# Linear attention and a rational feed-forward layer: the reciprocal in PSUM, ScalarE ahead of VectorE, low parts on GpSimd

## The chip, the cores and the metric

The kernel runs on one NeuronCore of a Trainium2 chip. A core has a matrix engine (TensorE, PE in the profile; PEld is its weight load), three elementwise engines (VectorE or DVE, ScalarE or ACT, GpSimd or POOL), and SyncE (SP), which here only issues transfers. SBUF is the working memory, PSUM the memory that TensorE writes to, in eight banks of 128 x 512 float32. Each engine runs its own instructions in order and waits for others on semaphores. The metric is the device time of one execution in microseconds (us); lower is better.

## The reference

Linear attention over 8 batches of 576 tokens and 8 heads of 64, RMS-normed, then a feed-forward layer whose activation is a rational function. `P / Q` is taken for each of 4608 x 2048 values of h.

```python
kv = np.einsum('bhsd,bhse->bhde', k, v)
out = np.einsum('bhsd,bhde->bhse', q, kv)
rms = np.sqrt(np.mean(out * out, axis=-1, keepdims=True) + 1e-06)
x = (out / rms * g_norm)            # then (B*S, H*D) = (4608, 512)
...
h = x @ w_in                        # 512 -> 2048
h2 = h * h
h3 = h2 * h
P = a[0] + a[1] * h + a[2] * h2 + a[3] * h3
Q = 1.0 + np.abs(b[0]) * np.abs(h) + np.abs(b[1]) * h2
g = P / (Q + 1e-06)
return g @ w_out                    # 2048 -> 512
```

## The kernel before

**Tiles and chunks.** The 4608 tokens are nine tiles of 512 (`t`), the 2048 columns of h are sixteen chunks of 128 (`c`). One chunk is: `gemm1` (h = w_in chunk times x, 128 x 512 in a PSUM bank of the pool `h`, two banks), the elementwise part `ew_a` to `ew_d`, and `gemm2` (g times the chunk of w_out, added into four banks `acc`). The main loop walks over all 144 chunks; chunk i issues `gemm2` of chunk i - 2 (`LAG`) and `gemm1` of chunk i + 1, so TensorE is one chunk ahead of the elementwise engines and takes their results two chunks later. `finish` does the last chunk in two halves and stores the last tile.

**Plain and split.** In tile 0 (and, for w_out, in chunks 12 to 15 of tile 1: `unsplit`, `LATE`) matmuls run on plain float32. Elsewhere every operand is split into a high part, cast to fp32r by ScalarE, and a low part, the difference, which VectorE computes; three fp32r matmuls (high x low, low x high, high x high) take the place of one plain one. So g has `gh`, `gl` (L461, L462), x has `xh`, `xl` (L268, L272), q has `qh`, `ql` (L307, L316), and the weights have `wh`, `wl` (L224, L231).

**Weights.** They come as float64 words. VectorE and ScalarE convert them in units of two chunks (`conv_a`, `conv_b1`, `conv_b2`) during tile 0, and `split_w` splits them from chunk 14 of tile 0 on. The table `schedule` says in which chunk, counted through from 0, each unit is fetched, converted and split (its four numbers); 33 and 35 are chunks 1 and 3 of tile 2.

**The elementwise part.** ScalarE takes Square of h, |b0 h| and the inner polynomial's first step from PSUM; VectorE makes Q - 1 (`q`, L429), then u (L431, L437); ScalarE makes an estimate d of the reciprocal as exp(-ln Q) (L438, L439); VectorE does a Newton step with it (L443, L445, L451), which gives g. The scale and shift constants are [128, 1] columns.

**The order.** It is the order in which the code is written, per engine (`manual_schedule`). `ew_b` and `ew_c` have places (`fill`, -1 to 2) where VectorE takes up other work: conversions and splits of weights, x's low parts, and the steps of the next tile's attention, which run one per chunk (`attention`: `att_kv`, `att_o`, then `att_ms`, `att_rstd`, `att_rd`, `att_rb`, `att_norm`). In chunk 14 of each tile x of the next tile is split. All fetches and nearly all stores are issued by SyncE. The eight PSUM banks are four `acc`, two `h`, one `at` and one `ms`.

Of the kernel before, what the change touches and what calls it, by code (L numbers as in the profile page):

```python
# [23 lines left out]
def linear_attention_then_rational_ffn(  # L24
# [189 lines left out]
    def split_w(u):  # L214
        kind, c = u
        i = units.index(u)
        w = ups.pop(u)
# [6 lines left out]
        ACT.copy(wh, w)  # L224

        def rest():
            wl = gpart(0, 0) if i == 0 else fpart(i if i == NU - 1 else i - 1, "l")
            for j in range(2):
# [2 lines left out]
            DVE.tensor_tensor(wl, w, f32(wh), ALU.subtract)  # L231
        return rest
# [189 lines left out]
    def ew_a(t, c, ph, w=TW):  # L422
        nm = f"{t}_{c}"
        d = work.tile([P, w], F32, tag="d", name=f"d_{nm}")
# [2 lines left out]
        ACT.activation(d, ph, AF.Square)  # L427
        ACT.activation(q, ph, AF.Abs, scale=b0)  # L428
        DVE.scalar_tensor_tensor(q, d, b1abs, q, ALU.mult, ALU.add)  # L429
        ACT.activation(u, ph, AF.Identity, bias=na[:, 2:3], scale=na[:, 3:4])  # L430
# [1 line left out]
        pend[t, c] = (d, q, u)

    def ew_b(t, c, ph, fill=lambda k: None):
        d, q, u = pend[t, c]
# [2 lines left out]
        ACT.activation(d, q, AF.Ln, bias=bias[:, 2:3], scale=QSC)  # L438
        ACT.activation(d, d, AF.Exp, bias=bias[:, 3:4], scale=-1.0)  # L439

    def ew_c(t, c, fill=lambda k: None):
        d, q, u = pend[t, c]
        DVE.scalar_tensor_tensor(q, q, QEPS, d, ALU.add, ALU.mult)  # L443
# [1 line left out]
        DVE.scalar_tensor_tensor(u, u, na[:, 0:1], d, ALU.add, ALU.mult)  # L445
# [5 lines left out]
        DVE.scalar_tensor_tensor(g, q, 2.0, u, ALU.subtract, ALU.mult)  # L451
        fill(2)

    def ew_d(t, c, w=TW):
        u = pend.pop((t, c))[2]
# [6 lines left out]
        DVE.tensor_tensor(gl, u, f32(gh), ALU.subtract)  # L462
# [211 lines left out]
```

## Time and profile before

| | us |
|---|---|
| median of 3 runs (lowest, highest) | 917.36 (917.17, 919.2) |
| span of the profiled execution, first to last instruction | 915.9 |
| busy: PE, DVE, ACT, POOL | 899.0, 800.2, 685.3, 4.6 |
| mean granted TensorE clock | 0.994 |

The page lists no time of the profiled execution other than its span; the three timed runs lie 1.3 to 3.3 us above it. A row of the timeline has the start, the length, the engine, the line, the operation and out<-in by the program's names; in brackets the idle time of the engine before it and what ended it. A row of the waits has who waited, for whom, and the total, the number and the longest. A group's row has the count, the busy time, the mean in ns, and the idle time before.

### The profile page before, as it was taken

What the parts mean: (1) busy time and instruction counts of PE and PEld (TensorE: products, weight loads), DVE (VectorE), ACT (ScalarE), POOL (GpSimd) and SP (SyncE); (2) the same over time, 40 slices, a digit from 0 to 9 for tenths busy, and PEclk for the clock granted to TensorE, in tenths of its full rate; (3) what the DMA queues carried; (4) which work ended last, traced back from release to release, by engine and by line L of the source; (5) the groups of instructions that cost most, each with busy time, mean ns of one, the idle gap of its engine ahead of it and who ended that gap; (6) DMA issues with size and microseconds to landing.
All of it is one profiled execution on the core that took longest, in us unless ns stands there. A gap on an engine that the chain in (4) does not pass through costs nothing.

```text
span 915.9 us, 11648 instructions
## 1 busy us (share of the span) xinstructions
PE 899.0 (98%) x4292; PEld 679.7 (74%) x4292; DVE 800.2 (87%) x1251; ACT 685.3 (75%) x1163; POOL 4.6 (1%) x32
## 2 busy tenths in 40 slices
PE   7999999999999999999999999999999999999998
PEld 5444445777678788878887888788887888788886
DVE  3799999999988899889987997889878988898887
ACT  2687866988687778777877787678867787777665
POOL 2000000000000000000000000000000000000000
PEclk7999999999999999999999999999999999999999
DMA  8946101221032013211221113120212020101001
GB/s 314 373 172 226 34 25 41 92 76 48 1 127 70 18 42 103 65 41 47 87 81 41 48 41 126 42 48 29 98 52 48 0 69 13 48 1 46 1 1 46
DMA packets 24992, 65.89 MB, mean 72 GB/s; under 512 B 2856, under 2 KB 3880, under 8 KB 24936
## 3 DMA queue, kind: packets, MB, share of 16 engines
q1 hardware_dynamic: 23328, 63.58, 21.5%
q10 hardware_dynamic: 1608, 1.58, 0.5%
q8 instruction: 33, 0.54, 0.3%
q14 instruction: 23, 0.19, 0.1%
HBM read 55.58 MB, written 9.57 MB: 71 GB/s over the span
## 4 chain that ended last, share of the span: by engine, by line
PE 83%; DVE 11%; ACT 3%; issue 2%; DMA 1%; ACTq 0%; DVEq 0%
PE h L417 13%; PE h L419 12%; PE h L418 12%; PE acc L478 11%; PE acc L479 11%; PE acc L480 11%; PE acc L474 3%; PE h L413 2%; PE kvp L301 2%; DVE q L429 1%; DVE u L445 1%; DVE q L443 1%; PE idle L533 1%; DVE u L437 1%; PE ms L345 1%
## 5 line engine op out<-in xcount | busy, mean ns | idle before, releaser
L427 ACT ACTIVATE d<-h 128x512 f32<-128x512 f32 x143 | 85.7, 599 | 160.6 <-PE h L419 146.9
L417 PE MATMUL h<-x,parts 128*128 128x512 f32 (+1 forms) x516 | 205.8, 399 | 0.0
L419 PE MATMUL h<-x,parts 128*128 128x512 f32 (+1 forms) x516 | 200.5, 389 | 0.0
L479 PE MATMUL acc<-wol,gh 128*128 128x512 f32 x492 | 191.6, 389 | 0.7 <-DVE wol L231 0.7
L429 DVE SCALAR_TENSOR_TENSOR q<-d,b1abs,q 128x512 f32<-128x512 f32 x143 | 107.1, 749 | 81.5 <-ACT q L428 81.2
L418 PE MATMUL h<-x,wil 128*128 128x512 f32 (+1 forms) x452 | 175.5, 388 | 0.0
L478 PE MATMUL acc<-parts,gl 128*128 128x512 f32 x440 | 171.6, 390 | 0.2 <-DVE gl L462 0.2
L480 PE MATMUL acc<-parts,gh 128*128 128x512 f32 x440 | 171.2, 389 | 0.0
L438 ACT ACTIVATE d<-q,bias 128x512 f32<-128x512 f32 x143 | 105.4, 737 | 29.9 <-DVE q L429 28.8
L417 PEld LDWEIGHTS h<-x,parts 128*128 128x128 f32 x516 | 96.9, 188 | 26.4 <-DVE gl L462 5.0
L419 PEld LDWEIGHTS h<-x,parts 128*128 128x128 f32 x516 | 96.9, 188 | 20.6
L430 ACT ACTIVATE u<-h,na 128x512 f32<-128x512 f32 x143 | 112.0, 783 | 0.0
L479 PEld LDWEIGHTS acc<-wol,gh 128*128 128x128 f32 x492 | 92.4, 188 | 20.0 <-DVE wol L231 1.0
L439 ACT ACTIVATE d<-d,bias 128x512 f32<-128x512 f32 x143 | 103.5, 724 | 4.6
L445 DVE SCALAR_TENSOR_TENSOR u<-u,na,d 128x512 f32<-128x512 f32 x143 | 106.5, 745 | 0.0
L437 DVE SCALAR_TENSOR_TENSOR u<-u,na,h 128x512 f32<-128x512 f32 x143 | 106.0, 741 | 0.3
L443 DVE SCALAR_TENSOR_TENSOR q<-q,d 128x512 f32<-128x512 f32 x143 | 98.4, 688 | 1.3 <-ACT d L439 1.3
L431 DVE TENSOR_TENSOR u<-u,h 128x512 f32<-128x512 f32 x143 | 97.8, 684 | 0.9
L428 ACT ACTIVATE q<-h,ab 128x512 f32<-128x512 f32 x143 | 98.1, 686 | 0.0
L418 PEld LDWEIGHTS h<-x,wil 128*128 128x128 f32 x452 | 85.0, 188 | 16.2 <-issue 0.2
L478 PEld LDWEIGHTS acc<-parts,gl 128*128 128x128 f32 x440 | 82.6, 188 | 18.5 <-DVE gl L462 1.1
L480 PEld LDWEIGHTS acc<-parts,gh 128*128 128x128 f32 x440 | 82.6, 188 | 17.1
(136 smaller groups left out, 1087.6 us busy)
## 6 DMA issues: line engine op xcount, KB each, us to landing
kvm<-in_kv_dram SPq DMA_DIRECT2D x28, 640.0 KB
raw_wo<-in_w_out_dram SPq DMA_DIRECT2D x8, 1024.0 KB
qr<-in_qT_dram SPq DMA_DIRECT2D x32, 256.0 KB
out_dram<-ob SPq DMA_DIRECT2D x16, 512.0 KB
rb<-rd SPq DMA_DIRECT2D x28, 256.0 KB
raw_wi<-in_w_in_dram SPq DMA_DIRECT2D x6, 1024.0 KB
first<-in_first_dram SPq DMA_DIRECT2D x4, 640.0 KB
raw_wi<-in_w_in_dram SPq DMA_DIRECT2D x4, 512.0 KB
```

Source lines behind the costliest of these rows:

```text
L417: PE.matmul(ph, wh, xl, start=(kc == 0), stop=False)
L418: PE.matmul(ph, wl, xh, start=False, stop=False)
L419: PE.matmul(ph, wh, xh, start=False, stop=(kc == NPAIR - 1))
L429: DVE.scalar_tensor_tensor(q, d, b1abs, q, ALU.mult, ALU.add)
L430: ACT.activation(u, ph, AF.Identity, bias=na[:, 2:3], scale=na[:, 3:4])
L437: DVE.scalar_tensor_tensor(u, u, na[:, 1:2], ph, ALU.add, ALU.mult)
L438: ACT.activation(d, q, AF.Ln, bias=bias[:, 2:3], scale=QSC)
L443: DVE.scalar_tensor_tensor(q, q, QEPS, d, ALU.add, ALU.mult)
L445: DVE.scalar_tensor_tensor(u, u, na[:, 0:1], d, ALU.add, ALU.mult)
L478: PE.matmul(o, gl[:, ss], wh, start=(c == 0), stop=False)
L479: PE.matmul(o, gh[:, ss], wl, start=False, stop=False)
L480: PE.matmul(o, gh[:, ss], wh, start=False, stop=(c == NF - 1))
```

## The change

- **Elementwise part.** q is now (|b1 h| + |b0|) h, whose absolute value is Q - 1. ScalarE reads h twice (|b1 h|, called v, and u), VectorE makes q from v and h, and ScalarE then takes Abs of q in SBUF, Ln and Exp. The old Square is gone.
- **The reciprocal r** has a PSUM bank of its own (`r_bank`, tag `r`), written by Ln and Exp; VectorE's Newton step reads and writes it there. `att_ms` moves from the bank `ms` to `at`.
- **Order in `ew_c`.** The first place for other work (`fill(0)`) now stands ahead of the first step that needs the reciprocal, and u is multiplied by r ahead of q.
- **GpSimd makes the low parts** `wl`, `ql` and `gl`. Those of x and of kv stay on VectorE.
- **w_out in tile 1** is split in all chunks: the last two units are split in chunks 12 and 14 of tile 1 (28 and 30).
- **The last copies** in `finish` get tiles of other tags for the second half of the output.

```diff
-    b1abs = const.tile([P, 1], F32, name="b1abs")
-    b0 = ab[:, 4:5]
+    b0abs = const.tile([P, 1], F32, name="b0abs")
+    b1 = ab[:, 5:6]
...
-        ("wo", 12): (6, 11, 12, 33),
-        ("wo", 14): (7, 12, 13, 35),
+        ("wo", 12): (6, 11, 12, 28),
+        ("wo", 14): (7, 12, 13, 30),
...
     def unsplit(t, c):
-        return t == 0 or t == 1 and c >= LATE
+        return t == 0
...
-            DVE.tensor_tensor(wl, w, f32(wh), ALU.subtract)
+            POOL.tensor_tensor(wl, w, f32(wh), ALU.subtract)
...
-                DVE.tensor_tensor(ql, q, f32(qh), ALU.subtract)
+                POOL.tensor_tensor(ql, q, f32(qh), ALU.subtract)
...
-        rs[t] = ps_at.tile([P, TW], F32, tag="ms", name=f"ms_{t}", bufs=1)
+        rs[t] = ps_at.tile([P, TW], F32, tag="at", name=f"ms_{t}", bufs=1)
...
     def ew_a(t, c, ph, w=TW):
...
-        ACT.activation(d, ph, AF.Square)
-        ACT.activation(q, ph, AF.Abs, scale=b0)
-        DVE.scalar_tensor_tensor(q, d, b1abs, q, ALU.mult, ALU.add)
+        ACT.activation(v, ph, AF.Abs, scale=b1)
         ACT.activation(u, ph, AF.Identity, bias=na[:, 2:3], scale=na[:, 3:4])
+        DVE.scalar_tensor_tensor(q, v, b0abs, ph, ALU.add, ALU.mult)
         DVE.tensor_tensor(u, u, ph, ALU.mult)
...
-    def ew_b(t, c, ph, fill=lambda k: None):
+    def ew_b(t, c, ph, r, fill=lambda k: None):
...
         fill(-1)
+        ACT.activation(q, q, AF.Abs)
         DVE.scalar_tensor_tensor(u, u, na[:, 1:2], ph, ALU.add, ALU.mult)
-        ACT.activation(d, q, AF.Ln, bias=bias[:, 2:3], scale=QSC)
-        ACT.activation(d, d, AF.Exp, bias=bias[:, 3:4], scale=-1.0)
+        ACT.activation(r, q, AF.Ln, bias=bias[:, 2:3], scale=QSC)
+        ACT.activation(r, r, AF.Exp, bias=bias[:, 3:4], scale=-1.0)
...
     def ew_c(t, c, fill=lambda k: None):
-        d, q, u = pend[t, c]
-        DVE.scalar_tensor_tensor(q, q, QEPS, d, ALU.add, ALU.mult)
+        q, u, r = pend[t, c]
         fill(0)
-        DVE.scalar_tensor_tensor(u, u, na[:, 0:1], d, ALU.add, ALU.mult)
+        DVE.scalar_tensor_tensor(u, u, na[:, 0:1], r, ALU.add, ALU.mult)
+        DVE.scalar_tensor_tensor(r, q, QEPS, r, ALU.add, ALU.mult)
         fill(1)
...
-        DVE.scalar_tensor_tensor(g, q, 2.0, u, ALU.subtract, ALU.mult)
+        DVE.scalar_tensor_tensor(g, r, 2.0, u, ALU.subtract, ALU.mult)
...
-        DVE.tensor_tensor(gl, u, f32(gh), ALU.subtract)
+        POOL.tensor_tensor(gl, u, f32(gh), ALU.subtract)
...
+    def r_bank(t, c):
+        return ps_at.tile([P, TW], F32, tag="r", name=f"r_{t}_{c}", bufs=1)
...
+        ends = (("d", 2), ("q", 2)), (("at", 4), ("rb", 2))
...
-                halves = [work.tile([P, DM // 2], F32, tag=e, name=f"ob{e}_{t}_{k}_{s}") for e in "dq"]
+                halves = [work.tile([P, DM // 2], F32, tag=e, name=f"ob{e}_{t}_{k}_{s}", bufs=b) for e, b in ends[k]]
...
-        ew_b(t, c, ph, lambda k: [f() for f in rest[k]])
+        ew_b(t, c, ph, r_bank(t, c), lambda k: [f() for f in rest[k]])
```

Three places show what this does to the order. The names end in the chunk and a buffer number (`h_14_898` is h of chunk 14). First VectorE in chunk 14 of tile 0, before; `x_0`, `x_2` are the low parts of tile 1's x, `parts_922` the low part of the first unit of w_in:

```order
L429 SCALAR_TENSOR_TENSOR q_14_912<-d_14_911,b1abs,q_14_912 128x512
L431 TENSOR_TENSOR u_14_913<-u_14_913,h_14_898 128x512
L437 SCALAR_TENSOR_TENSOR u_14_913<-u_14_913,na,h_14_898 128x512
L443 SCALAR_TENSOR_TENSOR q_14_912<-q_14_912,d_14_911 128x512
L272 TENSOR_TENSOR x_0_933<-xf_0_441,x_0_933 128x512
L445 SCALAR_TENSOR_TENSOR u_14_913<-u_14_913,na,d_14_911 128x512
L272 TENSOR_TENSOR x_0_933<-xf_1_528,x_0_933 128x512
L451 SCALAR_TENSOR_TENSOR g_14_943<-q_14_912,u_14_913 128x512
L231 TENSOR_TENSOR parts_922<-wiw_283,parts_922 128x1024
L272 TENSOR_TENSOR x_2_936<-xf_2_620,x_2_936 128x512
L272 TENSOR_TENSOR x_2_936<-xf_3_712,x_2_936 128x512
```

And the same chunk of the changed kernel:

```order
L428 SCALAR_TENSOR_TENSOR q_14_926<-v_14_925,b0abs,h_14_912 128x512
L429 TENSOR_TENSOR u_14_927<-u_14_927,h_14_912 128x512
L436 SCALAR_TENSOR_TENSOR u_14_927<-u_14_927,na,h_14_912 128x512
L271 TENSOR_TENSOR x_0_948<-xf_0_444,x_0_948 128x512
L444 SCALAR_TENSOR_TENSOR u_14_927<-u_14_927,na,r_14_932 128x512
L445 SCALAR_TENSOR_TENSOR r_14_932<-q_14_926,r_14_932 128x512
L271 TENSOR_TENSOR x_0_948<-xf_1_533,x_0_948 128x512
L451 SCALAR_TENSOR_TENSOR g_14_958<-r_14_932,u_14_927 128x512
L271 TENSOR_TENSOR x_2_951<-xf_2_627,x_2_951 128x512
L271 TENSOR_TENSOR x_2_951<-xf_3_721,x_2_951 128x512
```

The first low part of x now stands ahead of every step that needs the reciprocal, and the low part of w is gone from this engine. Second, GpSimd of the changed kernel from the same chunk to chunk 3 of tile 1 (before, it has nothing there); `wil` and `wol` are low parts of w_in and w_out:

```order
L230 TENSOR_TENSOR parts_937<-wiw_283,parts_937 128x1024
L315 TENSOR_TENSOR ql_0_1026<-qr_0_726,qh_0_1025 128x512
L230 TENSOR_TENSOR wil_1053<-wiw_294,parts_1008 128x1024
L462 TENSOR_TENSOR gl_0_1063<-u_0_998,gh_0_1062 128x512
L230 TENSOR_TENSOR wol_1113<-wow_326,parts_1008 128x1024
L230 TENSOR_TENSOR wil_1115<-wiw_373,parts_1072 128x1024
L462 TENSOR_TENSOR gl_1_1125<-u_1_1057,gh_1_1124 128x512
L315 TENSOR_TENSOR ql_1_1162<-qr_1_1030,qh_1_1161 128x512
L230 TENSOR_TENSOR wol_1189<-wow_419,parts_1072 128x1024
L462 TENSOR_TENSOR gl_2_1199<-u_2_1119,gh_2_1198 128x512
```

Up to two weights' parts stand ahead of a chunk's low part of g. Third, ScalarE in a chunk of the last tile, before (`gh_11` is the cast of the chunk before's g):

```order
L427 ACTIVATE d_12_7526<-h_12_7510 128x512
L428 ACTIVATE q_12_7527<-h_12_7510,ab 128x512
L430 ACTIVATE u_12_7528<-h_12_7510,na 128x512
L461 CAST gh_11_7534<-u_11_7485 128x512
L438 ACTIVATE d_12_7526<-q_12_7527,bias 128x512
L439 ACTIVATE d_12_7526<-d_12_7526,bias 128x512
```

And in the changed kernel:

```order
L426 ACTIVATE v_12_7710<-h_12_7694,ab 128x512
L427 ACTIVATE u_12_7712<-h_12_7694,na 128x512
L461 CAST gh_11_7717<-u_11_7668 128x512
L435 ACTIVATE q_12_7711<-q_12_7711 128x512
L437 ACTIVATE r_12_7721<-q_12_7711,bias 128x512
L438 ACTIVATE r_12_7721<-r_12_7721,bias 128x512
```

The number of passes is the same; one of them has moved from ahead of VectorE's q to behind it.

More of the change, by code (lines that the diff above doesn't have):

```diff
@@ L423, in ew_a @@
         nm = f"{t}_{c}"
[L424 removed]
+        v = work.tile([P, w], F32, tag="d", name=f"v_{nm}")
         q = work.tile([P, w], F32, tag="q", name=f"q_{nm}")
         u = work.tile([P, w], F32, tag="u", name=f"u_{nm}")
[L427 to L429 removed]
+        ACT.activation(v, ph, AF.Abs, scale=b1)
         ACT.activation(u, ph, AF.Identity, bias=na[:, 2:3], scale=na[:, 3:4])
+        DVE.scalar_tensor_tensor(q, v, b0abs, ph, ALU.add, ALU.mult)
         DVE.tensor_tensor(u, u, ph, ALU.mult)
[L432 to L435 removed]
+        pend[t, c] = (q, u)
+    def ew_b(t, c, ph, r, fill=lambda k: None):
+        q, u = pend[t, c]
         fill(-1)
+        ACT.activation(q, q, AF.Abs)
         DVE.scalar_tensor_tensor(u, u, na[:, 1:2], ph, ALU.add, ALU.mult)
[L438 to L439 removed]
+        ACT.activation(r, q, AF.Ln, bias=bias[:, 2:3], scale=QSC)
+        ACT.activation(r, r, AF.Exp, bias=bias[:, 3:4], scale=-1.0)
+        pend[t, c] = (q, u, r)
     def ew_c(t, c, fill=lambda k: None):
[L442 to L443 removed]
+        q, u, r = pend[t, c]
         fill(0)
[L445 removed]
+        DVE.scalar_tensor_tensor(u, u, na[:, 0:1], r, ALU.add, ALU.mult)
+        DVE.scalar_tensor_tensor(r, q, QEPS, r, ALU.add, ALU.mult)
         fill(1)
@@ L450, in ew_c @@
             g = u
-        DVE.scalar_tensor_tensor(g, q, 2.0, u, ALU.subtract, ALU.mult)
+        DVE.scalar_tensor_tensor(g, r, 2.0, u, ALU.subtract, ALU.mult)
         fill(2)
     def ew_d(t, c, w=TW):
-        u = pend.pop((t, c))[2]
+        u = pend.pop((t, c))[1]
         if (t, c) in gs:
@@ L499, in finish @@
         (ca, pa), (cb, pb) = parts
+        r = r_bank(t, c)
         ew_a(t, ca, pa, w)
         ew_d(t, c - 1)
-        ew_b(t, ca, pa)
+        ew_b(t, ca, pa, r[:, 0:w])
         gemm2(t, c - 2)
@@ L506, in finish @@
         ew_d(t, ca, w)
-        ew_b(t, cb, pb)
+        ew_b(t, cb, pb, r[:, w:])
         ew_c(t, cb)
@@ L555, in linear_attention_then_rational_ffn @@
     x0 = xpool.tile([P, NPAIR, TW], F32, tag="xB", name="x0")
-    idle = ps_at.tile([P, TW], F32, tag="ms", name="idle", bufs=1)
+    idle = ps_at.tile([P, TW], F32, tag="r", name="idle", bufs=1)
     ctx.enter_context(tc.manual_schedule())
@@ L569, in linear_attention_then_rational_ffn @@
         fetch_w(u)
-    ms0 = ps_at.tile([P, TW], F32, tag="ms", name="ms_0", bufs=1)
+    ms0 = ps_at.tile([P, TW], F32, tag="r", name="ms_0", bufs=1)
     for p in range(NPAIR):
@@ L581, in linear_attention_then_rational_ffn @@
     ACT.copy(x0[:, NPAIR - 1], o0[NPAIR - 1])
-    ACT.activation(b1abs, ab[:, 5:6], AF.Abs)
+    ACT.activation(b0abs, ab[:, 4:5], AF.Abs)
     conv_a(units[2])
     for p in range(NPAIR):
-        pool, tag, bufs = ((ps_h, "h", 2), (ps_h, "h", 2), (ps_at, "at", 1), (ps_at, "ms", 1))[p]
+        pool, tag, bufs = ((ps_h, "h", 2), (ps_h, "h", 2), (ps_at, "at", 1), (ps_at, "r", 1))[p]
         rb = pool.tile([P, TW], F32, tag=tag, name=f"rb_0_{p}", bufs=bufs)
```

1 line of the change is left out of this document (removed).

## The prediction

> **What bounds the kernel now.** The page first: its span, the busy time of each engine, and the chain that ended last.
>
> ```profile
> span 915.9 us, 11648 instructions
> PE 899.0 (98%) x4292; PEld 679.7 (74%) x4292; DVE 800.2 (87%) x1251; ACT 685.3 (75%) x1163; POOL 4.6 (1%) x32
> PE 83%; DVE 11%; ACT 3%; issue 2%; DMA 1%; ACTq 0%; DVEq 0%
> ```
>
> TensorE is busy 98% of the time and holds 83% of the chain; GpSimd is idle. Such shares are averages, so two stretches follow (columns: length, busy PE, PEld, DVE, ACT and POOL with their instructions, granted clock, DMA).
>
> ```profile
> 180.00:210.00 30.00, 29.78 (x167) 22.45 (x166) 29.26 (x44) 26.39 (x45) 0.00 (x0) 1.00 0.20 62
> 840.00:870.00 30.00, 30.00 (x134) 24.85 (x133) 25.77 (x41) 19.64 (x32) 0.00 (x0) 1.00 0.00 1
> ```
>
> In the last tile TensorE streams 134 matmuls in 30 us, 0.224 us each, without a pause, and VectorE has 4 us to spare: TensorE alone is the bound, and nothing that lightens VectorE can show. In tile 1 VectorE is full too. So time can come only from work that TensorE need not do, or from places where it waits. The list of waits names nearly all of these behind the start, and the waits of the last copies:
>
> ```profile
> PE op L327 <- DVE kvl L249: 1.9, 1, 1.9
> PE h L418 <- DVE parts L231: 1.6, 1, 1.6
> PE acc L479 <- DVE wol L231: 0.7, 1, 0.7
> ACT obd L519 <- DMA out_dram<-obd: 1.6, 2, 1.0
> DVE obq L519 <- DMA out_dram<-obq: 1.2, 1, 1.2
> ```
>
> TensorE waits 4.2 us, three times, each time for VectorE, and all before 170 us.
>
> **The change part by part.** The sums are made against the span of 915.9 us; the median of the runs is 917.36, so about 1.5 us lie around the span, and I add them at the end.
>
> *w_out split whole in tile 1.* The chain in order of time has four groups like these (the first and the last of them):
>
> ```profile
> 238.65 3.43 PE acc L474 x8
> 258.11 3.43 PE acc L474 x8
> ```
>
> A plain group (four matmuls, run as eight passes) takes 3.43 us. The split one takes 12 x 0.224 = 2.69. Four groups save 4 x 0.74 = **3.0 us** of TensorE's own work, the one part that shortens the bound directly. It brings four more casts of g on ScalarE and four more low parts; the two late splits of w_out are not new, only moved from tile 2 into tile 1.
>
> *ScalarE's chain.* One chunk of the last tile, where nothing else is in the way:
>
> ```profile
> 859.20 0.60 ACT L427 ACTIVATE d<-h 128x512 f32<-128x512 f32 x1 [1.71 <-PE h L419]
> 859.70 0.68 ACT L428 ACTIVATE q<-h,ab 128x512 f32<-128x512 f32 x1
> 860.93 0.63 ACT L461 CAST gh<-u 128x512 fp32r<-128x512 f32 x1
> 861.44 0.74 ACT L438 ACTIVATE d<-q,bias 128x512 f32<-128x512 f32 x1
> 862.21 0.73 ACT L439 ACTIVATE d<-d,bias 128x512 f32<-128x512 f32 x1
> 864.36 0.69 DVE L451 SCALAR_TENSOR_TENSOR u<-q,u 128x512 f32<-128x512 f32 x1
> 865.85 0.75 DVE L429 SCALAR_TENSOR_TENSOR q<-d,b1abs,q 128x512 f32<-128x512 f32 x1 [0.81 <-ACT q L428]
> ```
>
> Square goes, so all behind it starts 0.5 us earlier (859.20 to 859.70). An Abs from SBUF comes in between gh and Ln; the nearest row is the cast of gh, 0.63 long, so 0.65. Ln starts at 861.6 instead of 861.44, g ends at 865.2 instead of 865.05, and the next q (865.85 here), which now waits for one pass over h and not two, could start at 865.35. It just fits: TensorE's 24 matmuls a chunk, 5.4 us, hide it. Where VectorE is behind, the loop from q to q is q 0.75, Abs 0.6, Ln 0.77, Exp 0.75, then u, r and g at 0.65 to 0.7, together about 4.85 us, plus all that VectorE does between Exp and g. That is below 5.4, but catching up is slow. Behind the new Abs, which waits for q, stand Ln, Exp and the attention's casts.
>
> *The reciprocal in PSUM.* Reading PSUM on ScalarE is shown, writing it by ScalarE or VectorE is not:
>
> ```profile
> L438 ACT ACTIVATE d<-q,bias 128x512 f32<-128x512 f32 x143 | 105.4, 737 | 29.9 <-DVE q L429 28.8
> L254 ACT ACTIVATE r<-ms,bias 128x512 f32<-128x512 f32 x9 | 6.0, 672 | 1.1 <-PE ms L572 1.1
> L430 ACT ACTIVATE u<-h,na 128x512 f32<-128x512 f32 x143 | 112.0, 783 | 0.0
> ```
>
> Ln takes 737 ns out of SBUF and 672 out of PSUM, so a pass gains at best 65 ns; 783 is the longest pass of this width, so it loses at worst 46. I take zero, the plain Ln being the nearest row. One bank is enough: Ln of a chunk needs its q, and VectorE does that only after g of the chunk before. VectorE's passes cost 0.68 to 0.75 wherever they read, so I leave them.
>
> *Low parts on GpSimd.* The page has no subtraction there, only fills:
>
> ```profile
> L117 POOL MEMSET kvl<- 128x128 f32 x6 | 1.3, 214 | 0.1
> L85 POOL MEMSET kvf<- 128x1024 f32 x1 | 1.0, 951 | 0.0
> L462 DVE TENSOR_TENSOR gl<-u,gh 128x512 fp32r<-128x512 f32 x123 | 84.1, 684 | 0.0
> ```
>
> One stream costs 0.82 ns an element and 0.11 us. A subtraction moves three: at most 0.11 + 3 x 0.42 = 1.4 us for 512 columns and 2.6 for 1024; at least VectorE's own 0.68 and 1.22. I take the upper end. In chunks 1 to 8 of tile 1 GpSimd then has 11 parts of w and 12 of g and q, 45 us of about 50 (eight chunks of 5.4 and the attention's 0.9). The next fetch of q on SP's queue waits for GpSimd's low part of q, but has two chunks. Since g is used two chunks later, only two low parts are urgent: the first of w_out and the last of g.
>
> *The wait for kvl (1.9 us).* VectorE has been full since its first q:
>
> ```profile
> 35.70 0.75 DVE L429 SCALAR_TENSOR_TENSOR q<-d,b1abs,q 128x512 f32<-128x512 f32 x1 [1.13 <-ACT q L428]
> 37.99 0.69 DVE L443 SCALAR_TENSOR_TENSOR q<-q,d 128x512 f32<-128x512 f32 x1 [0.15 <-ACT d L439]
> ```
>
> That q starts 0.5 us earlier (one ScalarE pass ahead of it instead of two), and the wait for Exp goes because the conversion now stands ahead of it. VectorE's other work in tile 0 is the same. **-0.7 us.**
>
> *The change from tile 0 to tile 1 (1.6 us).*
>
> ```profile
> 141.75 1.03 ACT L224 CAST parts<-wiw 128x1024 fp32r<-128x1024 f32 x1
> 142.69 2.17 ACT L268 CAST x<-xf 128x512 fp32r<-128x512 f32 x4
> 145.81 1.22 DVE L231 TENSOR_TENSOR parts<-wiw,parts 128x1024 fp32r<-128x1024 f32 x1
> 146.94 1.29 DVE L272 TENSOR_TENSOR x<-xf,x 128x512 fp32r<-128x512 f32 x2
> 147.17 0.47 PE L418 MATMUL h<-x,parts 128*128 128x512 f32 x1 [1.56 <-DVE parts L231]
> ```
>
> w's low part stands behind g on VectorE and ends at 147.03. On GpSimd it starts when its high part is cast (142.8) and ends at 145.4. Then x's low parts set the end: VectorE does them 1.2 us earlier for w's part, but the first now stands ahead of the reciprocal and waits for Exp and a cast, some 0.6 later. **-1.0 us.** Of the third wait and smaller ones up to 200 us I count **-0.7**: VectorE loses 1.2 to 2.4 us a chunk there, but ScalarE, 26.4 of 30 us busy, becomes the next limit, and w_out's first low part takes twice as long on GpSimd.
>
> *Chunk 14 of tile 1.* The last split of w_out (a copy, a cast of 1.03) now stands on ScalarE ahead of the four casts of x (2.17) that tile 2 needs, and TensorE comes there 1.5 us sooner, two split groups being done. By the loop above (the first low part of x at 7.2 us behind h, the last at 11.7, TensorE wanting it at about 11) TensorE waits **+0.9 us**.
>
> *The end.*
>
> ```profile
> 908.98 0.41 ACT L461 CAST gh_15.5_7716<-u_15.5_7700 128x256 fp32r<-128x256 f32 x1 [1.40 <-DVE u_15.5_7700 L451]
> 909.90 0.50 PE L478 MATMUL acc<-woh,gl_15.5_7717 128*128 128x512 f32 x1 [0.23 <-DVE gl_15.5_7717 L462]
> 911.50 0.37 ACT L519 COPY obd<-acc 128x256 f32<-128x256 f32 x1 [1.04 <-DMA out_dram<-obd]
> 912.85 0.42 DVE L519 COPY obq<-acc 128x256 f32<-128x256 f32 x1 [0.33 <-ACT obd L519]
> ```
>
> The last half-chunk has no cover: two Abs of some 0.4 each and a low part that takes 0.3 longer put TensorE's last group 1.3 us later. With rooms of their own the last copies no longer wait for earlier stores; the last could start at 912.0 rather than 912.85. Together **+0.45 us**.
>
> Sum: -3.0 - 0.7 - 1.0 - 0.7 + 0.9 + 0.45 = -4.05; 911.85 us of span, **913.3** with what lies around it.
>
> **The rivals.**
>
> *GpSimd and VectorE get in each other's way.* The reciprocal in PSUM leaves VectorE's chunk work one SBUF operand each, but x's low parts and the norms of xf keep two, and they stand just where w's low parts run: chunk 14 of tile 0, chunks 12 and 14 of tile 1. If one blocks the other, x's first low part starts at 145.4 instead of 142.9 and the 1.0 us there is lost, and the wait in tile 1 grows from 0.9 to about 4.3 (norm 2.0 late in chunk 12, x 1.9 in chunk 14). Then the small gains of tile 1 go as well: about +0.9 in place of -4.05, or **918.3**. No row shows GpSimd beside VectorE, so nothing in this profile speaks against it. The Trainium skill, "SBUF — State Buffer", section "Who interferes with whom", says that a VectorE instruction with two SBUF inputs and a GpSimd one that reads SBUF exclude each other for the whole instruction; by that rule this rival is the result, while without it the forecast stands, and no run so far shows either. I give 0.25, half of it within 0.2%.
>
> *Everything is hidden.* The three waits go whole and the end costs nothing: -3.0 - 4.2 - 0.85 = -8.05, **909.3**. For it: GpSimd may be as quick as VectorE's row. Against it: ScalarE. 0.18.
>
> *The longer chain outruns TensorE (slower).* In chunks 11 to 15 five loops (24.3), four norms (2.7) and x's parts (3.1, with the wait for a cast) ask 30 us of VectorE against 27 of TensorE; the lag of two chunks hides this, with 0.2 us left at x's last low part. If PSUM or Abs add over 0.05 us a pass, five passes in four chunks put about 1.2 us on each of seven tile changes: +8, **921**. It decides from some 0.2 us of extra chain. 0.12.
>
> That the change would not do what it says is no rival: the listed instructions have the twelve split matmuls.
>
> **How the numbers follow.** The forecast has 0.45. What a measurement can tell from no change is about 0.2%, 1.8 us: faster is below 915.5, slower above 919.2. Faster: 0.42 of the forecast, 0.18 whole, 0.07 of the blocking case, 0.67. Within: 0.03, 0.12 and 0.04 of the others, 0.19. Slower: 0.14. The range from 908.8 to 919.0 leaves out most of the last rival.
>
> **What would show it.** TensorE's groups of w_out in tile 1 at 2.7 us with casts between; waits of h for low parts under 1 us at both tile changes (longer, with x's low parts on VectorE stretched to 2 us: blocking); GpSimd's subtractions near 1.4 and 2.6 us; and the tiles 2 to 7 as long as before, which the chain shows by the sums of squares, one a tile:
>
> ```profile
> 400.76 1.00 PE ms L345 x8
> 496.20 1.00 PE ms L345 x8
> ```
>
> These are 95.4 us apart (longer: the chain). The prediction is wrong if tiles 2 to 7 change at all, or if TensorE waits for x's parts at each tile change.

## The result, and the profile after

The changed kernel takes **928.75 us** (median of 4 runs, 928.51 to 928.79) against 917.4 before, a ratio of 1.0117 (95% interval 1.0103 to 1.0131): slower by 11 us, where 4 us less were forecast. The profiled execution has a span of 926.7, 10.8 more than before.

The page of the changed kernel: span, busy time of each engine, and the chain that ended last by engine.

```profile
span 926.7 us, 11878 instructions
PE 905.4 (98%) x4308; PEld 683.4 (74%) x4308; DVE 709.8 (77%) x1082; ACT 709.8 (77%) x1167; POOL 247.1 (27%) x205
PE 55%; DVE 23%; ACT 18%; issue 3%; DMA 1%; POOL 0%; POOLq 0%; ACTq 0%; DVEq 0%
```

VectorE did lose 90 us of work. But TensorE's share of the chain fell from 83% to 55%, and what it lost went to VectorE and ScalarE handing over to each other. The waits of the changed kernel (who waits for whom: total, times, longest) name the handover:

```profile
DVE u L444 <- ACT r L438: 89.4, 121, 0.7
DVE q L428 <- ACT u L427: 79.3, 70, 4.0
PE h L416 <- DVE x L271: 4.8, 5, 1.6
PE op L326 <- DVE kvl L248: 2.1, 1, 2.1
```

In 121 of 143 chunks VectorE stands 0.74 us before its first pass with the reciprocal, 89.4 us in all: as much as it lost in work (90.4). This alone shows no loss: where TensorE sets the pace, work that leaves VectorE comes back as idling. The run "holes" below shows where the idling costs time. The waits for the last copies' earlier stores are gone from the list; that for kvl is not shorter (1.9 before).

The sums of squares, one a tile, which the prediction named as the test:

```profile
406.67 1.00 PE ms L344 x8
502.61 0.99 PE ms L344 x8
```

They are 95.94 us apart, 95.44 before. So tiles 2 to 7 did change. The next table takes, from the traces, the start of TensorE's first row of h in a chunk (tile.chunk), in the kernel named less in the one before, and shows what was added from one place to the next. "Holes" and "best" are experiments below.

| stretch | predicted | after | holes | best |
|---|---|---|---|---|
| start to 0.5 | -0.7 | +0.1 | +0.1 | -0.8 |
| 0.5 to 0.6 | 0 | +1.7 | +1.6 | 0.0 |
| 0.6 to 1.1 | -1.0 | +2.4 | +0.6 | -0.7 |
| 1.1 to 1.14 | -0.7 | -1.3 | -0.3 | -1.9 |
| 1.14 to 2.2 (holds the -3.0 of w_out) | -2.1 | +2.6 | -1.0 | -1.2 |
| 2.2 to 8.3 | 0 | +4.6 | +0.3 | 0.0 |
| 8.3 to the end | +0.45 | +0.8 | +0.8 | -0.65 |
| sum | -4.05 | +10.8 | +2.1 | -5.3 |

Three things are to be read out of the trace of the changed kernel.

**GpSimd and VectorE.** Two places of the timeline, at the change from tile 0 to 1 and in chunk 12 of tile 1:

```profile
145.35 2.37 POOL L230 TENSOR_TENSOR parts<-wiw,parts 128x1024 fp32r<-128x1024 f32 x1 [131.47 <-ACT parts L223]
145.82 2.44 DVE L271 TENSOR_TENSOR x<-xf,x 128x512 fp32r<-128x512 f32 x1 [2.21 <-ACT x L267]
148.31 0.50 PE L416 MATMUL h<-x,parts 128*128 128x512 f32 x1 [1.15 <-DVE x L271]
...
236.35 2.39 POOL L230 TENSOR_TENSOR wol<-wow,parts 128x1024 fp32r<-128x1024 f32 x1 [1.77 <-ACT parts L223]
236.54 2.75 DVE L379 SCALAR_TENSOR_TENSOR xf<-xf,ghalf,rb 128x512 f32<-128x512 f32 x1
```

x's low part takes 2.44 us instead of 0.69 and ends 0.5 behind GpSimd's subtraction (147.72); the norm takes 2.75 instead of 0.75 and ends 0.55 behind it (238.74). Both read two operands from SBUF: they ran for the most part after GpSimd's subtraction and not beside it. This is the rule of the Trainium skill, "SBUF — State Buffer", section "Who interferes with whom", and the trace agrees. Of the sixteen low parts of w, three meet such a pass; the third time it is x's first low part at the change from tile 1 to 2 (2.45 us).

**The chain of a chunk.** One chunk of the last tile:

```profile
869.21 0.69 ACT L426 ACTIVATE v<-h,ab 128x512 f32<-128x512 f32 x1 [1.21 <-PE h L418]
869.79 0.77 ACT L427 ACTIVATE u<-h,na 128x512 f32<-128x512 f32 x1
870.60 0.75 DVE L428 SCALAR_TENSOR_TENSOR q<-v,b0abs,h 128x512 f32<-128x512 f32 x1 [0.49 <-ACT u L427]
871.38 0.63 ACT L435 ACTIVATE q<-q 128x512 f32<-128x512 f32 x1 [0.31 <-DVE q L428]
873.47 0.75 DVE L444 SCALAR_TENSOR_TENSOR u<-u,na,r 128x512 f32<-128x512 f32 x1 [0.74 <-ACT r L438]
874.86 0.69 DVE L451 SCALAR_TENSOR_TENSOR u<-r,u 128x512 f32<-128x512 f32 x1
```

q needs v, which ends at 869.90, but it starts at 870.60, when u ends (870.56): it waits for both of ScalarE's reads of h, 1.39 us behind the first. g (the last row) starts 5.65 behind it; before, q came 1.21 and g 5.16 behind the Square (859.20 and 864.36 in the prediction's rows; this is q's):

```profile
860.41 0.75 DVE L429 SCALAR_TENSOR_TENSOR q<-d,b1abs,q 128x512 f32<-128x512 f32 x1 [0.80 <-ACT q L428]
```

**VectorE's holes at a tile change.** Chunk 14 of tile 2, from its q to the next, and TensorE's weight load that waits for g's low part of that chunk:

```profile
344.38 0.74 DVE L428 SCALAR_TENSOR_TENSOR q<-v,b0abs,h 128x512 f32<-128x512 f32 x1
347.77 0.69 DVE L271 TENSOR_TENSOR x<-xf,x 128x512 fp32r<-128x512 f32 x1 [1.28 <-ACT x L267]
348.38 0.74 DVE L444 SCALAR_TENSOR_TENSOR u<-u,na,r 128x512 f32<-128x512 f32 x1
352.04 0.74 DVE L428 SCALAR_TENSOR_TENSOR q<-v,b0abs,h 128x512 f32<-128x512 f32 x1
353.33 0.19 PEld L481 LDWEIGHTS acc<-woh,gl 128*128 128x128 f32 x1 [0.54 <-POOL gl L462]
```

From q to q are 7.66 us, before 6.89:

```profile
338.41 0.74 DVE L429 SCALAR_TENSOR_TENSOR q<-d,b1abs,q 128x512 f32<-128x512 f32 x1
345.30 0.74 DVE L429 SCALAR_TENSOR_TENSOR q<-d,b1abs,q 128x512 f32<-128x512 f32 x1
```

In the changed kernel VectorE idles 1.28 us: Exp comes late, ScalarE's cast of x comes behind Exp, and with `fill(0)` moved ahead nothing stands there that could run. The pass at 348.38 needs only Exp and could have. TensorE then waits for g.

### The profile page after: what moved, and what is told of

It reads as the page before. It is cut to its first block, busy times and chain, and to the rows that moved or that the text cites. A ratio compares the mean times of both kernels' runs of the same rounds, so it can differ in the third digit from the quotient of the medians.

```text
span 926.7 us, 11878 instructions
## 1 busy us (share of the span) xinstructions
PE 905.4 (98%) x4308; PEld 683.4 (74%) x4308; DVE 709.8 (77%) x1082; ACT 709.8 (77%) x1167; POOL 247.1 (27%) x205
## 4 chain that ended last, share of the span: by engine, by line
PE 55%; DVE 23%; ACT 18%; issue 3%; DMA 1%; POOL 0%; POOLq 0%; ACTq 0%; DVEq 0%
PE h L416 8%; PE acc L481 7%; PE h L418 7%; PE acc L482 7%; PE h L417 7%; PE acc L483 7%; DVE q L428 5%; ACT r L437 4%; ACT q L435 4%; ACT r L438 4%; DVE r L445 3%; DVE u L451 3%; DVE xf L379 3%; DVE u L444 3%; PE h L412 2%
## 5 line engine op out<-in xcount | busy, mean ns | idle before, releaser
L462 POOL TENSOR_TENSOR gl<-u,gh 128x512 fp32r<-128x512 f32 x127 | 167.0, 1315 | 464.9 <-ACT gh L461 318.2
L482 PE MATMUL acc<-wol,gh 128*128 128x512 f32 x508 | 197.9, 390 | 0.5 <-POOL wol L230 0.5
L444 DVE SCALAR_TENSOR_TENSOR u<-u,na,r 128x512 f32<-128x512 f32 x143 | 106.8, 747 | 89.4 <-ACT r L438 89.4
L426 ACT ACTIVATE v<-h,ab 128x512 f32<-128x512 f32 x143 | 99.0, 692 | 92.6 <-PE h L418 82.5
L428 DVE SCALAR_TENSOR_TENSOR q<-v,b0abs,h 128x512 f32<-128x512 f32 x143 | 106.2, 743 | 79.5 <-ACT u L427 79.3
L435 ACT ACTIVATE q<-q 128x512 f32<-128x512 f32 x143 | 90.5, 633 | 56.6 <-DVE q L428 55.0
L461 ACT CAST gh<-u 128x512 fp32r<-128x512 f32 x127 | 79.2, 624 | 32.5 <-DVE u L451 32.5
L437 ACT ACTIVATE r<-q,bias 128x512 f32<-128x512 f32 x143 | 99.1, 693 | 4.7
L438 ACT ACTIVATE r<-r,bias 128x512 f32<-128x512 f32 (+1 forms) x145 | 95.6, 659 | 4.7
L445 DVE SCALAR_TENSOR_TENSOR r<-q,r 128x512 f32<-128x512 f32 x143 | 98.5, 689 | 0.0
```

The costliest lines, as they stand in the source:

```text
L428: DVE.scalar_tensor_tensor(q, v, b0abs, ph, ALU.add, ALU.mult)
L435: ACT.activation(q, q, AF.Abs)
L437: ACT.activation(r, q, AF.Ln, bias=bias[:, 2:3], scale=QSC)
L438: ACT.activation(r, r, AF.Exp, bias=bias[:, 3:4], scale=-1.0)
L444: DVE.scalar_tensor_tensor(u, u, na[:, 0:1], r, ALU.add, ALU.mult)
L462: POOL.tensor_tensor(gl, u, f32(gh), ALU.subtract)
```

## The experiments

The theories: *exclusion* (GpSimd's subtractions and VectorE's passes with two SBUF operands hold each other up), *chain* (g ends later behind h), and, as part of it, *holes* (VectorE waits where other work could stand). Line numbers are those of the changed kernel; some edits shift them by one. Times are medians, ratios those to the kernel before on the same chip. The runs were taken in groups on different chips, where the kernel before has medians from 917.4 to 918.8, so a difference between runs of different groups is good to about 1 us.

| run | change to | us | ratio, 95% interval |
|---|---|---|---|
| chain alone | before | 935.39 | 1.0185 (1.0170 to 1.0200) |
| low parts alone | before | 927.58 | 1.0101 (1.0086 to 1.0116) |
| w_out alone | before | 920.16 | 1.0021 (1.0011 to 1.0030) |
| rooms alone | before | 917.15 | 0.9991 (0.9982 to 1.0000) |
| w's parts back | after | 933.62 | 1.0168 (1.0153 to 1.0183) |
| x's part only | after | 923.79 | 1.0048 (1.0035 to 1.0061) |
| holes | after | 919.78 | 1.0011 (1.0002 to 1.0020) |
| new chain, w on VectorE | holes | 925.92 | 1.0078 (1.0061 to 1.0095) |
| old chain, w on GpSimd | holes | 918.84 | 1.0001 (0.9993 to 1.0010) |
| old chain, w on VectorE | holes | 913.10 | 0.9947 (0.9931 to 0.9964) |
| the same, w_out as before | holes | 914.97 | 0.9963 (0.9952 to 0.9975) |
| the same as 913.10, reciprocal in SBUF | holes | 924.65 | 1.0064 (1.0051 to 1.0077) |
| the same as 913.10, order: best | holes | 912.48 | 0.9932 (0.9920 to 0.9944) |
| chain alone, holes filled | before | 930.00 | 1.0126 (1.0110 to 1.0142) |

### Each part alone on the kernel before

Chain alone: the change, with its new order in `ew_c`, but with these lines taken back (the low part of q and the last copies are taken back likewise).

```diff
-            POOL.tensor_tensor(wl, w, f32(wh), ALU.subtract)
+            DVE.tensor_tensor(wl, w, f32(wh), ALU.subtract)
...
-        POOL.tensor_tensor(gl, u, f32(gh), ALU.subtract)
+        DVE.tensor_tensor(gl, u, f32(gh), ALU.subtract)
...
+        ("wo", 12): (6, 11, 12, 33),
+        ("wo", 14): (7, 12, 13, 35),
+        return t == 0 or t == 1 and c >= 12
```

> The kernel before with the new element-wise chain alone (two reads of h ahead of q, Abs, the reciprocal in PSUM); all low parts stay on VectorE, w_out's late splits and the last copies stay as before. Chain theory (the change's loss comes from g ending 0.5 us later in each chunk, which each tile change and the end pay): the 0.5 us at each of six or seven tile changes, about 1.5 in the last two tiles and 0.8 at the end stay, some +5 to +6, so 922 to 924. Exclusion theory (the loss comes from GpSimd's subtractions and VectorE's passes with two SBUF operands holding each other up): GpSimd does nothing here, so 917 to 919. If the half clock after the wait at 63.7 us belongs to the chain, 1.7 us of the loss are here too.

935.39: far beyond both. The same table of stretches gives +4.1 from 1.1 to 1.14 and **+8.1 from 2.2 to 8.3**, 1.2 at each tile change. So the chain, with its order, loses time in tiles 2 to 7 with no GpSimd in play. It costs 4.1 in tile 1, where VectorE is full, and 2.6 from 0.6 to 1.1, of which 1.7 is a fall of the clock (told of at the end).

Low parts alone: the three `DVE.tensor_tensor` of `wl`, `ql` and `gl` become `POOL.tensor_tensor`.

> The kernel before with its low parts (w, q of the attention, g) moved to GpSimd and nothing else; the element-wise chain keeps four passes with both operands in SBUF. Exclusion theory: each low part of g (1.3 us on GpSimd) stands beside the passes r, u and g of VectorE and one holds up the other, so that a chunk of VectorE gets longer by up to 1.3 less the 0.68 that moved; in chunks 10 to 15 VectorE has no such room, so several us per tile, 930 to 960. Chain theory (no exclusion): VectorE gets 0.68 us a chunk lighter, TensorE is the bound, 913 to 918.

927.58, just under the range of the exclusion theory. In the trace of this kernel a pass that reads two SBUF operands, q or the last one (L451), takes 2.7 to 2.9 us beside twelve of the 13 low parts of w in tile 1; here it is q:

```profile
184.13 2.73 POOL L231 TENSOR_TENSOR wol<-wow,parts 128x1024 fp32r<-128x1024 f32 x1
184.53 2.89 DVE L429 SCALAR_TENSOR_TENSOR q<-d,b1abs,q 128x512 f32<-128x512 f32 x1
```

Of the 10.4 us in the span, 8.9 fall between 1.1 and 1.14, 1.6 are a fall of the clock at 62 to 70 us, and 0.0 fall between 2.2 and 8.3: in the later tiles TensorE hides the exclusion, so it is a matter of tiles 0 and 1 only.

w_out alone: `("wo", 12)` and `("wo", 14)` at 28 and 30, and `unsplit` only for `t == 0`.

> The kernel before with w_out split whole in tile 1 and nothing else (low parts on VectorE). TensorE has 4 x 0.74 = 3.0 us less to do. If VectorE and ScalarE can carry the two earlier splits and four more low parts of g there, 914.4. Exclusion theory expects this, about 914 to 916, since the 5.5 us that TensorE waits in chunks 12 of tile 1 to 1 of tile 2 of the changed kernel come from GpSimd beside VectorE. If the earlier splits alone are what is too much there (each 1.2 of VectorE and 1.0 of ScalarE in chunks 12 and 14, beside x's parts), TensorE waits 3 us or more and the time is 917 to 920.

920.16, the second case. TensorE's 3.0 us less are there, but from 1.14 to 2.2 the net is +1.95: it waits there for x's and g's low parts, with no GpSimd in play. Its profile also holds one fall of the clock, told of at the end.

Rooms alone: the change's `ends` in `finish`.

> The kernel before with rooms of their own for the last copies and nothing else. All theories: the waits of 1.6 and 1.2 us for earlier stores go, the last copy starts 0.85 us earlier, 916.5; if the store that follows is what sets the end, 917.4.

917.15, -0.9 against the kernel before in that group (918.03), and 0.76 less from 8.3 to the end: as predicted (0.85).

### On the changed kernel: w's parts back, and the holes

W's parts back: `DVE.tensor_tensor(wl, ...)`.

> The changed kernel with w's low parts (128x1024) back on VectorE; the low parts of g and of q stay on GpSimd. Exclusion theory: the passes that stood still beside them (x's first low part 2.44 us, one norm 2.75) come back to 0.69 and 0.75, and of the roughly 5.5 us that TensorE waits between chunk 12 of tile 1 and chunk 1 of tile 2 some 3 go, of the 2.4 at the change from tile 0 to 1 some 1: 923 to 926. Against it: VectorE gets 11 x 1.2 us more to do in tile 1; if load and not exclusion is what makes it late there, 928.5 or more.

A miss for the exclusion theory: 933.62, 5 us slower, though the norms take 0.745 us on average again (0.818 in the changed kernel) and x's parts 0.718 (0.794). The loss lies in tile 1 (2.6 us more from 1.1 to 1.14, 1.9 more from 1.14 to 2.2): VectorE's 1.2 us for each of w's parts cost more than the exclusion did, the other case of the expectation. In this kernel, taking the exclusion away alone gains nothing.

Holes:

```diff
-    fillat = {att_norm: 1, ...
+    fillat = {att_norm: 0, ...
...
         DVE.scalar_tensor_tensor(u, u, na[:, 0:1], r, ALU.add, ALU.mult)
+        fill(3)
         DVE.scalar_tensor_tensor(r, q, QEPS, r, ALU.add, ALU.mult)
...
-                rest[k].append(xl[k])
+                rest[(3, 1)[k]].append(xl[k])
```

> The changed kernel with two of VectorE's steps moved into its waits: the norms stand ahead of the first pass that needs Exp (where VectorE waits 0.74 us in each chunk) and x's first low part stands behind that pass instead of ahead of it (where VectorE waits 1.28 us). Nothing else. If the loss of 0.5 us at each tile change comes from these holes, chunks 11 to 14 get 0.6 to 0.75 us shorter each, the 0.5 goes seven times (3.5 us) and a part of the waits in tile 1 with it: 922 to 925.5. If it comes only from the later g of each chunk (0.5 us behind h, by q's wait for u and by Abs), the tile changes stay as they are: 927.5 to 929.

919.78: **9 us back for two moved steps**, more than expected. The timeline of chunk 12 of tile 1, of x's first part after it, and two of the sums of squares:

```profile
233.20 0.75 DVE L379 SCALAR_TENSOR_TENSOR xf<-xf,ghalf,rb 128x512 f32<-128x512 f32 x1
235.09 2.41 POOL L230 TENSOR_TENSOR wol<-wow,parts 128x1024 fp32r<-128x1024 f32 x1 [1.82 <-ACT parts L223]
...
245.93 2.41 POOL L230 TENSOR_TENSOR wol<-w_last,woh 128x1024 fp32r<-128x1024 f32 x1 [1.81 <-ACT woh L223]
246.40 2.48 DVE L271 TENSOR_TENSOR x<-xf,x 128x512 fp32r<-128x512 f32 x1 [0.76 <-ACT x L267]
```

```profile
401.76 1.00 PE ms L344 x8
497.20 1.00 PE ms L344 x8
```

The norm now ends before w's low part begins, so a filled hole also took it out of GpSimd's way (0.75 instead of 2.75); x's part still stands still. The sums of squares are 95.44 apart again, as before the change: the holes were the loss of tiles 2 to 7.

X's part only: the same without the line of the norms.

> The changed kernel with x's first low part behind the first pass that needs Exp and nothing else; the norms stay where the change has them. In chunk 14 of each tile VectorE then does that pass in the time in which it waited for the cast of x: some 0.65 us less. If this is the hole that sets the tile changes (chunk 14 grew by 0.78 us with the change, chunk 13 by 0.29), the 0.5 us goes at each of seven changes and some 0.6 at the change from tile 1 to 2: 924 to 925.5. If the norms' hole matters as much, about half of the 9 us of both together stays: 924 is then the upper part's share, and anything above 926.5 says the norms were the main part.

923.79, just below the expected range: x's part gives 5 us, the norms 4 (4.7 and 4.0 by the spans). From 2.2 to 8.3 the 4.6 fall to 1.7, and to 0.3 with the norms; at 1.14 to 2.2, 2.6 falls to 1.9, and to -1.0 with the norms.

### Old or new chain, w's parts on either engine

The first kernel below has, on "holes", the old chain with its estimate in the PSUM bank, w's parts on VectorE, and w_out as before; the second is the same with w_out split whole.

```diff
-        ACT.activation(v, ph, AF.Abs, scale=b1)
-        DVE.scalar_tensor_tensor(q, v, b0abs, ph, ALU.add, ALU.mult)
+        ACT.activation(v, ph, AF.Square)
+        ACT.activation(q, ph, AF.Abs, scale=b0)
+        DVE.scalar_tensor_tensor(q, v, b1abs, q, ALU.mult, ALU.add)
...
-        ACT.activation(q, q, AF.Abs)
```

> The chain of before (Square, Abs, q from both; no second Abs), with the reciprocal in PSUM, the low parts of g and q on GpSimd, those of w on VectorE, the holes filled as in the run beside it, w_out's late splits as before, own rooms for the last copies. Chain theory and exclusion theory agree that every cost found so far is gone: tiles 2 to 7 as before, tile 1 with 0.68 us a chunk less on VectorE: 914.5 to 917. If the low parts of g on GpSimd hold up q (its two operands lie in SBUF) in the chunks where VectorE is late, tile 1 gets longer and the time is 918 to 922.

> The kernel of the run beside it, with w_out split whole in tile 1 as in the change (late splits in chunks 12 and 14). TensorE has 3.0 us less to do. Split alone on the kernel before cost 2 us net, since x's and g's low parts on VectorE came late in chunks 12 to 15 of tile 1; here VectorE has 0.68 us a chunk less there, about 2.7 in all. If that lateness was VectorE's load, the wait falls from about 5 to 2.5 us and the time is 1 us or more below the run beside it: 913 to 916. If ScalarE's casts (w's, then x's four) set it, no gain: 917 to 919.

914.97 and 913.10, both as expected, and both faster than the kernel before. Splitting w_out whole takes 1.9 us off the median here; on the kernel before it lost. In the traces only 0.6 of it lies where the split acts (1.14 to 2.2); 1.0 is a fall of the clock at 62 to 70 us that the first profiled execution has and the second has not.

> The fastest kernel so far (old chain, reciprocal in PSUM, holes filled, w_out split whole; 913.1) with w's low parts on GpSimd instead of VectorE. It differs from the changed kernel with filled holes (919.8) in the chain alone, and from the 913.1 in the engine of w's low parts alone. Exclusion theory: q of the old chain has both operands in SBUF, so beside a low part of w (2.4 us) it stands still as it did in the run with all parts on GpSimd (0.75 became 2.89): eleven such in tile 1, 918 to 922. Without exclusion VectorE has 13 us less to do in tile 1: 911 to 913. Chain theory: whatever lies below 919.8 here beyond tile 1 is the price of the second Abs and of q's wait for u; about 1.5 us at the end.

918.84: 5.7 slower than with w's parts on VectorE, the exclusion theory's case: 5.1 of it lie between 1.1 and 1.14, and q takes 1.5 to 2.7 us beside nine of the low parts of w in tile 1. Meanwhile, between the two chains on GpSimd there is only 0.9. It left open what the new chain costs where w's parts are on VectorE:

> The changed kernel with filled holes and w's low parts on VectorE; it differs from the 913.1 kernel in the chain alone (new here, old there). If the chain itself costs nothing once the holes are filled, 913 to 915. If it costs by its length (g 0.5 us later behind h, VectorE waiting for Exp in each chunk of tile 1 without attention work to put there, the last half chunk 1 us longer): 919 to 922. Against the 919.8 of the same kernel with w's low parts on GpSimd, it gives the price of that engine in the new chain, whose q has one operand in PSUM: below 919.8, exclusion (two x parts of 2.4 us) outweighs VectorE's load; above, the load does.

925.92, beyond the upper case. So the four are:

| | w's parts on GpSimd | on VectorE |
|---|---|---|
| new chain | 919.8 | 925.9 |
| old chain | 918.8 | 913.1 |

The new chain costs 12.8 us where w's parts fill VectorE, and 0.9 where GpSimd takes them. In the traces the 12.8 are 12.4, and 3.4 of these are two falls of the clock that only the new chain's profiled execution has. Its q has one operand in PSUM and goes past GpSimd (all 143 in the changed kernel take 731 to 749 ns), the old one has two in SBUF and stands still: the chain pays for itself only by avoiding a collision that the move to GpSimd had made. What it costs is the same wait, by groups of one shape, first in the new chain with w on VectorE, then in the old:

```profile
L444 DVE SCALAR_TENSOR_TENSOR u<-u,na,r 128x512 f32<-128x512 f32 x143 | 106.8, 747 | 80.1 <-ACT r L438 79.0
```

```profile
L444 DVE SCALAR_TENSOR_TENSOR u<-u,na,r 128x512 f32<-128x512 f32 x143 | 106.5, 745 | 26.9 <-ACT r L438 23.2
```

79 us of idle VectorE against 23. Most of that is hidden by TensorE (from 2.2 to 8.3 the new chain loses 0.3 here). Between 1.1 and 2.2, where VectorE is full, VectorE stands 9.9 us before this pass against 1.9, and the new chain takes 6.1 us longer. Last, how much of the chain's 17 us on the kernel before are holes:

> The kernel before with the new chain alone (935.4) and the same two steps moved into VectorE's waits. All low parts are on VectorE, so the low part of g already fills most of the wait for Exp (0.26 us are left of 0.74), and the norms gain little; x's first low part gains some 0.65 in chunk 14 of each tile. If holes are the loss: 1.2 us at each of six tile changes fall to 0.5 or less and the time to 928 to 931. If the chain's length and VectorE's load in tile 1 are: 933 or more.

930.00, the case of the holes: 5.4 of 17.4. Of the 8.1 us from 2.2 to 8.3 go 5.1, and 3.0 stay there. From 0.6 to 1.1 go 2.0, 1.7 of them because the clock does not fall there now; from 1.1 to 1.14 the loss grows from 4.1 to 5.5. So the two steps are a third of it on that kernel. The rest fits the chain's length and VectorE's load, which no run separates.

### The reciprocal in PSUM, and the order of the low parts

Reciprocal in SBUF: on the 913.10 kernel, Ln, Exp and the pass after them write the tile `v`.

```diff
-        pend[t, c] = (q, u)
+        pend[t, c] = (v, q, u)
...
-        q, u = pend[t, c]
+        r, q, u = pend[t, c]
```

> The same 913.1 kernel with the reciprocal back in SBUF (Ln, Exp and the pass after them write the tile that the Square left), all else equal. Exclusion theory: u, r and g then have two operands in SBUF each, and GpSimd's low part of g (1.3 us) lands on them; in tiles 2 to 7 TensorE hides that (it did in the run with all parts on GpSimd), in tile 1, where VectorE is full, four chunks or more pay up to 0.6 each: 914.5 to 917. If the bank of the reciprocal brings nothing: 912.5 to 913.7.

924.65: without the bank the kernel is **11.5 us** slower, far more than the range. In the profiled executions it is 9.4, and 1.7 of that is a fall of the clock between 144 and 156 us that the 913.10 kernel's has not. In its timeline one of the passes with the estimate now stands beside GpSimd's low part of q, for 1.67 us instead of 0.69:

```profile
201.18 1.30 POOL L315 TENSOR_TENSOR ql<-qr,qh 128x512 fp32r<-128x512 f32 x1 [1.00 <-ACT qh L306]
201.36 1.67 DVE L446 SCALAR_TENSOR_TENSOR v<-q,v 128x512 f32<-128x512 f32 x1
```

From 2.2 to 8.3 nothing changes (0.0); 8.5 of the 9.4 us more in the span come before that, in tiles 0 and 1. From 1.1 to 2.2 it is 6.0: the passes with the estimate are 3.3 us longer there in all, and q 5.3. The pass q has both operands in SBUF in both kernels, but only here do GpSimd's low parts of g hold it up: five of these passes take 1.77 to 1.86 us instead of 0.75.

Order: on the 913.10 kernel, the last unit's low part behind x's, and the first unit's in two halves with the second behind x's.

```diff
-            rest[2].append(split_w(u))
+            (seconds if u == units[-1] else rest[2]).append(split_w(u))
...
+        rest[2] += seconds
+        seconds.clear()
```

> The 913.1 kernel with two low parts of w moved behind x's on VectorE: the second half of the first w_in unit's in chunk 14 of tile 0, and the last w_out unit's in chunk 14 of tile 1. TensorE waits 1.9 us at the first and 1.2 + 0.9 at the second place for x's low parts behind these. If it is VectorE's order there, 0.5 and 1.2 us go: 911 to 912.2; if it is ScalarE's casts, 913.

**912.48**, a little above the range, and 0.7% faster than the kernel before: the lowest median of all. The 0.6 below the 913.10 are no more than runs of different groups can tell apart. In the traces the first place gains 0.5, as expected. At the second TensorE's waits for x's parts (1.00 and 0.73) are gone, but one of 1.21 for g's low part from GpSimd stands in their place, and 0.6 are lost between 1.1 and 1.14.

## Why the prediction was wrong

- **TensorE is the bound, and the four split groups save 3.0 us.** Right: where nothing waits, from 2.1 to 2.2, the changed kernel gains 0.73 on a group (0.74 predicted).
- **"The next q ... now waits for one pass over h and not two": failed.** It waits for two, 1.39 us behind ScalarE's first read of h instead of 0.7: for v, and for u, which reads the same h and stands ahead of q (why it waits for u was not tried). With Abs at 0.63 (0.65 predicted) g comes 0.49 later and not 0.15.
- **"It just fits: TensorE's 24 matmuls a chunk, 5.4 us, hide it": the step that failed most.** The loop of 4.85 us was nearly right (4.95 from q to the end of g in the chunk shown), and in the last tile it is hidden. But the working took VectorE's lost work as time gained. It came back as 0.74 us of idling in 121 chunks, at places where the order puts nothing. Chunk 14 needed 0.77 us more from q to q, which the prediction had counted once, at the change from tile 0 to 1 ("some 0.6 later"), and not for the later tiles, where the same lines run. Cost: 4.6 us from 2.2 to 8.3, where nothing was forecast; with the holes filled 0.3 are left.
- **"x's low parts set the end ... -1.0", "+0.9" in chunk 14 of tile 1: failed.** The first place came to +2.4, 1.7 of it by a fall of the clock behind these waits (below); the second, with w_out's gain in it, to +2.6 against -2.1. The rival had named the places, x's first part at the first, a norm and x's part in tile 1, and 4.3 us of waits there; the rows of TensorE between 242 and 256 us wait 3.6 (0.55, 0.31, 1.62, 0.89, 0.23). The stretched passes are there, but they are not shown to be the loss: "chain alone" loses as much at the first place without GpSimd, filled holes bring it from 2.4 to 0.6 with x's part still stretched (2.44), and "w's parts back", without the exclusion of w's parts, is slower.
- **GpSimd's durations** were right: 1.315 us and 2.40 measured, 1.4 and 2.6 taken. It was the company that was costed wrong.
- **The reciprocal in PSUM at nothing:** right as a duration, even a little better, as these groups of the changed kernel show (means in ns: 693 and 662 for Ln and Exp, 737 and 724 before; 689 for VectorE's pass that writes it):

```profile
L437 ACT ACTIVATE r<-q,bias 128x512 f32<-128x512 f32 x143 | 99.1, 693 | 4.7
L438 ACT ACTIVATE r<-r,bias 128x512 f32<-128x512 f32 x143 | 94.7, 662 | 4.7
L445 DVE SCALAR_TENSOR_TENSOR r<-q,r 128x512 f32<-128x512 f32 x143 | 98.5, 689 | 0.0
```

  But its worth is mostly the exclusion that it avoids: in the kernel where it was taken away 11.5 us by the medians, 7.7 in the traces without the fall of the clock.
- **The wait for kvl, -0.7:** missed, 2.1 us against 1.9. It rested on the same step as q's one pass over h. The wait is 2.11 to 2.12 us in all seven kernels with the new chain, 1.75 to 1.76 in the four with the old chain and the estimate in PSUM, and 1.95 in the kernel before.
- **The end, +0.45:** +0.8. The rooms gave their 0.76 (0.85 predicted); so the last half chunk cost about 1.6 (0.82 + 0.76) and not 1.3.
- **The rivals** were given 0.25 and 0.12 as if one of them had to be chosen. Both effects came, and their prices add: 913.3 + 5.0 (918.3 - 913.3) + 7.7 (921 - 913.3) = 926.0. That this comes near 928.75 is luck: the sizes do not fit place by place (4.6 us from 2.2 to 8.3, where the longer chain had 1.2 at each tile change), and 3.4 of the 10.8 us are falls of the clock. The longer chain's condition did not hold either: Ln and Exp got shorter in PSUM, and Abs was as long as assumed. (The blocking case's own terms, -3.0 - 0.7 + 4.3 + 0.45, give +1.05 and not +0.9.) A range for a change of four parts has to hold the case in which two fail together.

## What to carry to other kernels

Work that leaves an engine is worth nothing if the engine then waits for the same chain: look, for each place in its order, what it can do while the chain runs, and put the independent steps there. Before GpSimd takes over a subtraction, list the VectorE passes with two operands in SBUF that will stand beside it; giving one of them a PSUM bank, or keeping the long subtractions on VectorE, decided the sign here. And what was found to be late at one tile change is to be counted at each of them.
